# Loading W1 in three pieces, two scalings on ScalarE, logarithms recorded behind their sums, and matmuls of a group's halves ahead of its products

## The chip, the core and the metric

The kernel runs on one core of a Trainium2 chip. Its time is the device time of one execution in microseconds; lower is better. Before the change three runs gave 902.16, 903.32 and 903.46 us, median 903.32. The profile is of a fourth execution that took 901.05 us, of which the profiler's span covers 899.2 us.

## What is computed

`x` is 8 x 4224 tokens of 192 channels, `weight_gen` 8 x 4224 x 8 heads x 7 taps. W1 is 192 x 768 and W2 768 x 192, both in float64 words.

```python
w = exp(weight_gen - max(weight_gen, -1)); w = w / (sum(w, -1) + 1e-9)      # softmax over 7 taps
y[b, s, h] = sum_k w[b, s, h, k] * x_padded[b, s + k, h]                     # causal conv, 24 channels a head
xn = (y - mean(y)) / sqrt(var(y) + 1e-6) * g_ln                             # over 192 channels
out = y + maximum(xn @ w_ch1, 0) @ w_ch2
```

## The kernel before

**Tiling.** A partition holds 264 consecutive tokens of one sequence, so one token column is 128 tokens. Columns are worked off in parts of 4, 8 or 12 (six parts of 4 come first), each part in chunks of 4 or 6 columns for the convolution and in groups of 4 columns for the two matrix products: 66 groups.

**A chunk.** VectorE multiplies shifted `x` by the softmax weights, two taps at a time into `pr` (L423) or one into `y`. Two of the pairs are folded by accumulating DMAs that GpSimd issues (L429), and GpSimd adds the four remaining arrays into `y` (L426). ScalarE then sums and squares each column (L463, L468), takes the root by a logarithm and an exponential (L491 to L493), VectorE refines it (L496 to L502), ScalarE scales (`xh`, L514), rounds to float16 (L530), and GpSimd makes the low half (L532). Both halves of a group are `hl`; one DMA on the SP queue transposes them into `xT` (L536).

**A group on TensorE.** Three units of 16 + 4 matmuls of 256 columns (L546) give the hidden layer in a PSUM tile `ph` (there are two). A unit's 4 "narrow" matmuls stand in an instruction group of their own, shared by two units. ScalarE takes the positive part (`hh`, L576), VectorE the low half (`hlo`, L578), and TensorE multiplies by W2 in four output columns `o0` to `o3` of 18 matmuls each (L615 to L617). The outputs of a group stand between the units of the next group. VectorE adds them to `y` (L628), and a DMA writes the chunk.

**Softmax.** Its weights, sums (`sm`, written at L368) and some helper columns all lie in one PSUM tile, `wn`. ScalarE reads the sums for the logarithm (L372, "log" below) and turns it into a reciprocal (L373), VectorE refines that (L378, L379) and multiplies (L384). There are 23 softmax blocks.

**Weights.** W1's first 128 rows come by one DMA into `hh0`, its last 64 rows by another into `hh1` with a pattern of two column halves, 64 rows, 768 words (L660), W2 by a third into a `pr` buffer (L666). VectorE and ScalarE turn the words into float32 (L686 to L702); a matmul against ones gives the norm (L709), and from it come the scalings `gi` of W1 (L754) and `fs` of the output (L800). `gi` is needed for the float16 halves of W1 (L764, L767), which twelve small DMAs spread over partitions (L770).

**What sets the order.** Every operation is recorded with an engine, a cost, a due time (`WANT`) and its reads and writes. `Plan.order` places one after another, and the kernel's instructions are issued in the order of the starts it found, engine by engine in order. Waits between engines are derived from the order in which the instructions are issued; two instructions of different engines on one PSUM tile are kept apart even if both only read. DMAs of SP and ScalarE share eight semaphores in turn (DMAHW0 to DMAHW7); one waits until the transfer that used its semaphore before has landed.

Of the kernel before, what the change touches and what calls it, by code (L numbers as in the profile page):

```python
# [12 lines left out]
ALU = mybir.AluOpType  # L13
# [10 lines left out]
CHUNK = 6  # L24
RING = 36
HALF = 512
TINY = struct.unpack("<f", struct.pack("<I", (1023 - 126) << 20))[0]


# [35 lines left out]
class Plan:  # L65
# [42 lines left out]
    def order(self):  # L108
        tenant = {p: [None] * len(t) for p, t in self.pools.items()}
        free, cand, dma_free, out = {}, {}, {}, []  # L110

        last, clear = {"add": None, "turn": None}, {"add": 0.0, "turn": 0.0}
        for o in self.ops:
            o.left = len(o.deps)
            for d in o.deps:
                d.nxt.append(o)
            cand.setdefault(o.eng, [])
            free[o.eng] = 750.0
            if not o.left:
                cand[o.eng].append(o)  # L120

        def vacant(b):
            at = []
            for i, t in enumerate(tenant[b.pool]):
                if t is None:
                    at.append((0.0, i))
                elif all(x.end is not None for x in t.ops):
                    at.append((max(x.end for x in t.ops), i))
            return min(at) if at else None

        def earliest(o):
            t = max(free[o.eng], o.ready)
            if o.kind in clear:
                t = max(t, clear[o.kind])
            for b in o.bufs:
                if b.slot is None:
                    v = vacant(b) if b.ops[0] is o else None
                    if v is None:
                        return None
                    t = max(t, v[0])  # L140
            return t


        for o in reversed(self.ops):
            for d in o.deps:
                d.want = min(d.want, o.want)
        by_want, lead = sorted(self.ops, key=lambda o: o.want), 0
        while len(out) < len(self.ops):
            pick = None
            while by_want[lead].start is not None:  # L150
                lead += 1
            until, near = by_want[lead].want + WINDOW, by_want[lead].want + NEAR
            for e, c in cand.items():
                rows = [(t, o) for t, o in ((earliest(o), o) for o in c
                                          if o.want <= (near if o.kind == "load" else until))
                        if t is not None]
                if rows:
                    t0 = min(t for t, _ in rows) + AHEAD
                    row = min((r for r in rows if r[0] <= t0), key=lambda r: (r[1].want, r[1].rank))
                    if pick is None or row[0] < pick[0]:  # L160
                        pick = row
            assert pick is not None, "nothing can be placed"
            t, o = pick
            for b in o.bufs:
                if b.slot is None:
                    b.slot = vacant(b)[1]
                    tenant[b.pool][b.slot] = b
            o.start = t
            free[o.eng] = t + o.cost
            o.end = t + o.cost + o.lat  # L170
            if o.dma:

                begin = max(t + o.cost + self.DMA_START[o.kind if o.kind == "turn" else o.eng],
                            dma_free.get(o.eng, 0.0))
                dma_free[o.eng] = begin + o.dma * (1.0 if o.kind == "turn" else 1.2)
                o.end = dma_free[o.eng] + self.DMA_END
            if o.kind in clear:
                other = "turn" if o.kind == "add" else "add"
                o.behind, last[o.kind] = last[other], o
                clear[other] = max(clear[other], o.end)  # L180
            cand[o.eng].remove(o)
            for x in o.nxt:
                x.left -= 1
                x.ready = max(x.ready, o.end - (o.lat if x.eng == o.eng == "PE" else 0.0))
                if not x.left:
                    cand[x.eng].append(x)
            out.append(o)
        return sorted(out, key=lambda o: (o.start, o.rank))


@with_exitstack
def kernel(
# [66 lines left out]
    def a_ns(n, more=93):  # L259
        return n / 1.2 + more  # L260
# [28 lines left out]
        s0 += n  # L289
    parts, chunks, s0 = [], [], 0  # L290
    for n in PARTS:
        pa = dict(S=s0, n=n, chunks=[], xT={})
        o = 0
        while o < n:
            m = min(CHUNK, n - o) if n % CHUNK == 0 else min(4, n - o)
            so = max((q for q in softs if q["S"] <= s0 + o), key=lambda q: q["S"])
            assert s0 + o + m <= so["S"] + so["n"] and (s0 + o) // RING == (s0 + o + m - 1) // RING
            ch = dict(S=s0 + o, o=o, n=m, part=pa, so=s0 + o - so["S"])
            chunks.append(ch)
            pa["chunks"].append(ch)  # L300
            o += m
        parts.append(pa)
        s0 += n
# [40 lines left out]
    def softmax(pa):  # L344
# [9 lines left out]

        sm = WN[:, S0_ : S0_ + m]

        def step(eng, cost, name, fn, r, w):
            op(eng, cost, (name, S0), fn, r, w)

        step("V", v_ns(m * K), "max",  # L360
             lambda: V.tensor_reduce(out=at(mx)[:, :m], in_=a3(), axis=AX.X, op=ALU.max), [wb], [mx])
# [10 lines left out]
            A.activation(at(rr)[:, :m], sm, AF.Ln, bias=bias[:, 1:2])  # L372
            A.activation(at(rr)[:, :m], at(rr)[:, :m], AF.Exp, scale=-1.0)  # L373

        step("ACT", 2 * a_ns(m, 180), "rcp", ln, ["sm"], [rr])

        def newton():
            V.scalar_tensor_tensor(out=sm, in0=sm, scalar=1e-9, in1=at(rr)[:, :m], op0=ALU.add, op1=ALU.mult)  # L378
# [74 lines left out]
    def norm(pa):  # L453
# [52 lines left out]

        for g in range(0, n, NT):
            xh, hl, xT = Buf("xh"), Buf("hl"), Buf("xT")
            pa["xT"][g] = xT

            def scaled(j, g=g, xh=xh):
                for t in range(j, j + 2):
# [53 lines left out]
    def at_unit(unit):  # L566
        gp, u = unit
        return gp["s"] + u * NT / 3

    def evict(unit):  # L570
# [11 lines left out]
        if gp["prev"]:  # L582
            for t in ((0,), (1,), (2, 3))[u]:
                output(gp["prev"], t, gp["s"])

    def products(a, b):
        for gp, u in (a, b):
            gp["ph"][u] = Buf("ph")
        xs = [a[0]["xT"], b[0]["xT"]]
        pa_, pb_ = (gp["ph"][u] for gp, u in (a, b))  # L590
        op("PE", 1744, ("unit", at_unit(a)), lambda: wide_products(*a, True), [xs[0], *W1S], [pa_], lat=420.0)
        op("PE", 640, ("narrow", at_unit(b)), lambda: narrow_products(a, b), [*xs, *W1S], [pa_, pb_], lat=80.0)
        evict(a)
        op("PE", 1744, ("unit", at_unit(b)), lambda: wide_products(*b, False), [xs[1], *W1S], [pb_], lat=420.0)
        evict(b)
# [55 lines left out]
    def words(i, o, n):  # L651
        return at(raw[i]).bitcast(I32).rearrange("p a b d -> p (a b d)" if i == 2 else "p j q -> p (j q)")[:, o : o + n]

    def load_weights():

        def dma(eng, E, want, dst, src, n, w):
            op(eng, 450, ("w_" + want, 0), lambda: E.dma_start(dst(), src), w=[w], dma=dma_ns(n), kind="load")

        dma("SP", SY, "load", lambda: words(0, 0, 2 * F), w1b[0:P, :], 8 * F, raw[0])
        dma("SP", SY, "load", lambda: words(1, 0, F),  # L660
            bass.AP(tensor=w1b.tensor, offset=P * 2 * F, ap=[[F, 2], [2 * F, 64], [1, F]]), 4 * F, raw[1])
        dma("ACT", A, "load", lambda: W["g"][:, 0:1], gcol[0:P, :], 200, "g0")
        for h, rows in (("t", top), ("b", bot)):
            dma("ACT", A, "load", lambda rows=rows: W["g"][rows, 1:2], gcol[P:D, :], 100, "g1" + h)
        wv2 = w2b.rearrange("(j p) d -> p j d", p=P)
        dma("SP", SY, "load2", lambda: words(2, 0, 2 * NF * D).rearrange("p (j d) -> p j d", d=2 * D), wv2,  # L666
            8 * NF * D, raw[2])
# [60 lines left out]
    def weights():  # L728
# [9 lines left out]
            return at(b).bitcast(F32).rearrange("p j q -> p (j q)")[:, o : o + n]  # L738

        from_double("a", lambda: words(0, 0, 2 * F), lambda: f32(wa, F), F, s1[:, 0:1], [raw[0]], [wa])  # L740
        from_double("c", lambda: words(1, 0, F), lambda: f32(wc, F2), F2, s1[:, 1:2], [raw[1]], [wc])
        want = ("w_s1", 0)

        def gsum():
# [5 lines left out]

        op("V", 580, want, gsum, [(wa, "sq"), (wc, "sq"), "g0", "g1t", "g1b"], ["s1"])
        w_scale("s1", s1[:, 2:3], 128.0, r1, ["s1"], "r1")
        op("V", 130, want,
           lambda: V.tensor_scalar(out=gi, in0=g, scalar1=r1[:, 2:3], scalar2=None, op0=ALU.mult),  # L754
           ["r1"], ["gi"])


# [34 lines left out]
        for h in range(3):  # L792
# [3 lines left out]
        op("V", 70, want2, lambda: V.tensor_reduce(out=s2[:, 3:4], in_=s2[:, 0:3], axis=AX.X, op=ALU.add),  # L796
           [((w2r, h), "sq") for h in range(3)], ["s2"])
        w_scale("s2", s2[:, 3:4], 16384.0, r2, ["s2"], "r2")
        op("V", 130, want2,
           lambda: V.scalar_tensor_tensor(out=W["fs"], in0=r1[:, 1:2], scalar=1.0 / ALPHA, in1=r2[:, 1:2],  # L800
                                          op0=ALU.mult, op1=ALU.mult), ["r1", "r2"], ["fs"])
        w2f, w2g = (a.rearrange("p j d -> p (j d)") for a in (w2h, w2l))
        wv = [(w2r, h) for h in range(3)]
        op("ACT", a_ns(NF * D, 186), want2,
# [23 lines left out]
    prev, units = None, []  # L828
    for pa in parts:
        for g in range(0, pa["n"], NT):  # L830
            prev = dict(hh=Buf("hh"), hlo=Buf("hlo"), pa=pa, g=g, s=pa["S"] + g, xT=pa["xT"][g], ph={}, prev=prev)
            units += [(prev, u) for u in range(3)]
    for a, b in zip(units[::2], units[1::2]):
        products(a, b)
# [37 lines left out]
```

## Time and profile before

| | |
|---|---|
| runs | 902.16, 903.32, 903.46 us |
| profiled execution | 901.05 us, span 899.2 us |
| TensorE (PE) | 813.2 us busy, 90% |
| VectorE (DVE) | 781.7 us, 87% |
| GpSimd (POOL) | 694.4 us, 77% |
| ScalarE (ACT) | 675.7 us, 75% |
| granted TensorE clock, mean | 0.991 of full speed |

All five engines work most of the time, so the share of busy time says little by itself. What a place is worth is read from the stretch: before 53 us TensorE has nothing to multiply; after 82 us it hardly ever stands.

### The profile page before, as it was taken

To read this page: it belongs to the slowest core of one execution; us is meant where nothing else is said; L and a number is where in the kernel's file an instruction comes from. 1 tells how busy PE (TensorE), PEld (TensorE's weight loads), DVE (VectorE), ACT (ScalarE), POOL (GpSimd) and SP (SyncE) were. 2 spreads that over 40 slices of the span, in tenths; PEclk is the share of its full clock that TensorE was granted. 3 is DMA by queue.
4 is the path that set the end of the run, shared out by engine and by line. 5 is a ranking of instruction groups with operands and counts; after the bars stand their busy time and mean duration, and the time that the engine had idled before them with its cause. 6 is when DMAs were issued, how large, how long until landed. Compare 5 with 4: busy or idle time off the path is not lost.

```text
span 899.2 us, 21468 instructions
## 1 busy us (share of the span) xinstructions
PE 813.2 (90%) x8716; PEld 728.8 (81%) x8716; DVE 781.7 (87%) x833; ACT 675.7 (75%) x1773; POOL 694.4 (77%) x403
## 2 busy tenths in 40 slices
PE   0037979999999999989999999999999999999997
PEld 0025969889898888888899988898899898889987
DVE  5799989999999999889999998999999799785332
ACT  1579877888878787788878778788788778788321
POOL 4499989998998896886987979689698598886000
PEclk9997999999999999999999999999999999999999
DMA  8875778878786878777788688787877867654212
GB/s 212 211 166 126 173 160 180 195 163 189 164 195 111 203 147 193 184 158 166 164 187 185 139 182 175 169 197 158 170 167 148 170 134 162 153 111 98 63 53 54
DMA packets 138604, 142.42 MB, mean 158 GB/s; under 512 B 107657, under 2 KB 109449, under 8 KB 138505
## 3 DMA queue, kind: packets, MB, share of 16 engines
q1 hardware_dynamic: 123513, 89.14, 42.0%
q0 software_dynamic: 14688, 51.91, 29.6%
q8 instruction: 68, 1.11, 0.5%
q14 instruction: 31, 0.25, 0.1%
q10 hardware_dynamic: 304, 0.00, 0.0%
HBM read 36.43 MB, written 25.95 MB: 69 GB/s over the span
## 4 chain that ended last, share of the span: by engine, by line
PE 26%; DVE 12%; POOL 9%; ACT 8%; DMA 6%; issue 5%; SPq 0%; POOLq 0%; DVEq 0%
PE ph L546 13%; POOL y L426 7%; DVE pr L423 7%; PE po L615 5%; PE po L617 4%; PE po L616 4%; DMA xT<-hl 3%; DVE hlo L578 3%; ACT hh L576 3%; ACT junk L468 2%; DMA pr<-pr 2%; ACT junk L463 1%; DVE y L423 1%; POOL hl L532 1%; DVE y L628 1%
## 5 line engine op out<-in xcount | busy, mean ns | idle before, releaser
L426 POOL TENSOR_TENSOR y<-y,pr 128x1152 f32<-128x1152 f32 (+1 forms) x204 | 503.6, 2475 | 82.0 <-DVE pr L423 70.5
L616 PE MATMUL po<-c_w2l,hh 128*128 128x192 f16 x1584 | 389.7, 246 | 1.4 <-POOL c_w2l L808 1.4
L615 PE MATMUL po<-c_w2h,hh 128*128 128x192 f16 x1584 | 390.1, 246 | 0.0
L617 PE MATMUL po<-c_w2h,hlo 128*128 128x192 f16 x1584 | 389.7, 246 | 0.0
L546 PE MATMUL ph<-xT,c_w1h 128*128 128x256 f16 x2376 | 328.3, 275 | 34.2 <-DMA xT<-hl 18.8
L423 DVE TENSOR_TENSOR pr<-x,wn 128x2304 f32<-128x2304 f32 (+1 forms) x153 | 337.4, 2215 | 8.3 <-DMA x<-in_x_dram 3.3
L546 PEld LDWEIGHTS <-c_w1h 128*128 128x128 f16 x2376 | 226.4, 98 | 76.4 <-issue 43.2
L578 DVE SCALAR_TENSOR_TENSOR hlo<-ph,hh 128x1024 f16<-128x1024 f32 x198 | 239.3, 1217 | 49.9 <-ACT hh L576 48.7
L576 ACT ACTIVATE hh<-ph 128x1024 f16<-128x1024 f32 x198 | 199.6, 1008 | 68.8 <-PE ph L546 46.0
L546 PE MATMUL ph<-xT,c_w1l 128*128 128x256 f16 (+1 forms) x1584 | 211.0, 274 | 9.8 <-DMA xT<-hl 8.9
L615 PEld LDWEIGHTS <-hh 128*128 128x128 f16 x1584 | 155.0, 98 | 7.8 <-issue 6.1
L616 PEld LDWEIGHTS <-hh 128*128 128x128 f16 x1584 | 155.1, 98 | 1.6
L617 PEld LDWEIGHTS <-hlo 128*128 128x128 f16 x1584 | 155.0, 98 | 1.6 <-issue 1.6
L514 ACT ACTIVATE xh<-y,s 128x192 f32<-128x192 f32 x264 | 123.3, 536 | 31.9 <-DVE s L502 28.3
L546 PEld LDWEIGHTS <-c_w1l 128*128 128x128 f16 (+1 forms) x1584 | 108.5, 96 | 41.8 <-issue 26.2
L532 POOL TENSOR_TENSOR hl<-xh,hl 128x768 f16<-128x768 f32 x66 | 118.8, 1868 | 15.9 <-ACT hl L530 15.8
L463 ACT ACTIVATE junk<-y 128x192 f32<-128x192 f32 x264 | 95.1, 360 | 42.4 <-POOL y L426 36.8
L468 ACT ACTIVATE junk<-y,s 128x192 f32<-128x192 f32 x264 | 119.5, 453 | 7.1
L429 POOL DMA_DIRECT2D pr<-pr x102 | 96.2, 1003 | 34.5 <-DVE pr L423 20.9
L628 DVE SCALAR_TENSOR_TENSOR y<-po,c_fs,y 128x384 f32<-128x384 f32 x132 | 79.8, 608 | 28.2 <-PE po L617 28.1
L530 ACT ACTIVATE hl<-xh 128x768 f16<-128x768 f32 x66 | 55.1, 835 | 8.2 <-DMA xT<-hl 7.6
L423 DVE TENSOR_TENSOR y<-x,wn 128x1152 f32<-128x1152 f32 (+1 forms) x51 | 60.0, 1178 | 0.0
(64 smaller groups left out, 327.2 us busy)
## 6 DMA issues: line engine op xcount, KB each, us to landing
pr<-pr POOLq DMA_DIRECT2D x60, 576.0 KB, 7.6
x<-in_x_dram SPq DMA_DIRECT2D x30, 576.0 KB, 7.0
out_dram<-y SPq DMA_DIRECT2D x30, 576.0 KB, 4.8
pr<-pr POOLq DMA_DIRECT2D x42, 384.0 KB, 6.6
out_dram<-y SPq DMA_DIRECT2D x21, 384.0 KB, 4.3
x<-in_x_dram SPq DMA_DIRECT2D x20, 384.0 KB, 6.6
w<-in_weight_gen_dram SPq DMA_DIRECT2D x21, 336.0 KB, 4.3
pr<-in_moe_w_ch_dram SPq DMA_DIRECT2D x1, 1152.0 KB
```

The lines of the kernel that those rows point to most:

```text
L423: V.tensor_tensor(out=ov, in0=xv, in1=wv, op=ALU.mult)
L426: E.tensor_tensor(out=flat(0), in0=flat(0), in1=flat(k), op=ALU.add)
L463: A.activation(junk, at(y)[:, j, :], AF.Identity, scale=-1.0 / D, accum_out=at(s4)[:, 3, t : t + 1])
L468: A.activation(junk, at(y)[:, j, :], AF.Square, bias=at(s4)[:, 3, t : t + 1], accum_out=at(s4)[:, 0, t : t + 1])
L514: A.activation(at(xh)[:, t, :], at(y)[:, i, :], AF.Identity, bias=at(s4)[:, 3, g + t : g + t + 1], scale=at(s4)[:, 1, g + t : g + t + 1])
L532: lambda xh=xh, hl=hl: Q.tensor_tensor(out=halves(hl, True), in0=pairs(xh), in1=halves(hl, False), op=ALU.subtract),
L546: T_.matmul(at(gp["ph"][u])[:, r, v * 2 * P : (v + 1) * 2 * P], W[w][rows, wb, (2 * u + v) * P : (2 * u + v + 1) * P], xv[rows, r, xb, :, ...
L576: lambda: A.activation(at(hh)[:, us, :], at(ph), AF.Relu), [ph], [(hh, u)])
L578: lambda: V.scalar_tensor_tensor(out=at(hlo)[:, us, :], in0=at(ph), scalar=0.0, in1=at(hh)[:, us, :], op0=ALU.max, op1=ALU.subtract),
L615: T_.matmul(o, tok(hh, j), w2h[:, j, :], start=(j == 0), stop=False)
L616: T_.matmul(o, tok(hh, j), w2l[:, j, :], start=False, stop=False)
L617: T_.matmul(o, tok(hlo, j), w2h[:, j, :], start=False, stop=(j == NF - 1))
```

## The change

Six edits, in the order of the diff: (1) in the placed order, everything that neither the log needs nor its engine runs ahead of it is recorded behind the log instead of ahead of it (`hoist`); (2) logs are marked for that; (3) before the first unit of each of the first six groups TensorE multiplies the group's untransposed halves, 14 matmuls whose results are overwritten; (4) W1's last 64 rows come by two DMAs of 64 partitions; (5) `gi` moves from VectorE to ScalarE; (6) `fs` moves from VectorE to ScalarE, as two instructions.

```diff
+FILLED = 24
@@ Plan.order
-        return sorted(out, key=lambda o: (o.start, o.rank))
+        out.sort(key=lambda o: (o.start, o.rank))
+        return self.hoist(out)
+
+    @staticmethod
+    def hoist(out):
+        for o in [o for o in out if o.kind == "next"]:
+            j = out.index(o)
+            i = max(out.index(d) for d in o.deps) + 1
+            first, rest, tenants = [o], [], {(b.pool, b.slot) for b in o.bufs}
+            need, engines = set(o.deps), {o.eng}
+            for x in reversed(out[i:j]):
+                if x in need or x.eng in engines or x.dma or any((b.pool, b.slot) in tenants for b in x.bufs):
+                    first.append(x)
+                    need |= x.deps
+                    engines.add(x.eng)
+                    tenants |= {(b.pool, b.slot) for b in x.bufs}
+                else:
+                    rest.append(x)
+            out[i : j + 1] = first[::-1] + rest[::-1]
+        return out
@@ softmax
-        step("ACT", 2 * a_ns(m, 180), "rcp", ln, ["sm"], [rr])
+        step("ACT", 2 * a_ns(m, 180), "rcp", ln, ["sm"], [rr], kind="next")
@@ products
+    def fill(gp, u):
+        if gp["s"] >= FILLED:
+            return [], lambda: None
+
+        def mm():
+            h = at(gp["hl"]).rearrange("p t a d -> p (t a d)")
+            for i in range(14):
+                T_.matmul(at(gp["ph"][u])[:, i % 2, : 2 * P], h[:, :P], h[:, 2 * P : 4 * P], start=True, stop=True)
+
+        return [(gp["hl"], 0), (gp["hl"], 1)], mm
...
-        op("PE", 1744, ("unit", at_unit(a)), lambda: wide_products(*a, True), [xs[0], *W1S], [pa_], lat=420.0)
-        op("PE", 640, ("narrow", at_unit(b)), lambda: narrow_products(a, b), [*xs, *W1S], [pa_, pb_], lat=80.0)
+        (fa, mma), (fb, mmb) = (fill(*x) if x[1] == 0 else ([], lambda: None) for x in (a, b))
+        def wide():
+            mma()
+            wide_products(*a, True)
+        def narrow():
+            mmb()
+            narrow_products(a, b)
+        op("PE", 1744, ("unit", at_unit(a)), wide, [xs[0], *W1S, *fa], [pa_], lat=420.0)
+        op("PE", 640, ("narrow", at_unit(b)), narrow, [*xs, *W1S, *fb], [pa_, pb_], lat=80.0)
@@ load_weights
-        dma("SP", SY, "load", lambda: words(1, 0, F),
-            bass.AP(tensor=w1b.tensor, offset=P * 2 * F, ap=[[F, 2], [2 * F, 64], [1, F]]), 4 * F, raw[1])
+        for h, rows in enumerate((top, bot)):
+            dma("SP", SY, "load", lambda rows=rows: words(1, 0, F)[rows],
+                bass.AP(tensor=w1b.tensor, offset=P * 2 * F + h * F, ap=[[2 * F, 64], [1, F]]), 2 * F, (raw[1], h))
@@ weights
-        op("V", 130, want,
-           lambda: V.tensor_scalar(out=gi, in0=g, scalar1=r1[:, 2:3], scalar2=None, op0=ALU.mult),
+        op("ACT", 230, want, lambda: A.activation(gi, g, AF.Copy, scale=r1[:, 2:3]),
            ["r1"], ["gi"])
...
-        op("V", 130, want2,
-           lambda: V.scalar_tensor_tensor(out=W["fs"], in0=r1[:, 1:2], scalar=1.0 / ALPHA, in1=r2[:, 1:2],
-                                          op0=ALU.mult, op1=ALU.mult), ["r1", "r2"], ["fs"])
+        def final_scale():
+            A.activation(W["fs"], r1[:, 1:2], AF.Copy, scale=1.0 / ALPHA)
+            A.activation(W["fs"], W["fs"], AF.Copy, scale=r2[:, 1:2])
+
+        op("ACT", 440, want2, final_scale, ["r1", "r2"], ["fs"])
```

The due times are unchanged, but with other costs and one more operation the planner places many operations otherwise. The orders of all engines differ in small swaps up to about TensorE's instruction 6,228 of 17,428 (some 370 us into the run) and agree behind it.

On the SP queue at the start, before the change (`hh0` and `hh1` are the two parts of W1, `w` the softmax inputs, `pr2` is W2; the brackets name what is waited for):

```order
L657 DMA hh0_88<-in_moe_w_ch1_dram 128x1536
L657 DMA hh1_89<-in_moe_w_ch1_dram 128x1x768
L341 DMA w0_64<-in_weight_gen_dram 128x1x672 [waits DMAHW1_49,DMAHW0_49,Pool_49]
L335 DMA x_63<-in_x_dram 128x1x768 [waits DMAHW3_49]
L335 DMA x_63<-in_x_dram 128x1x768 [waits DMAHW4_49]
L335 DMA x_63<-in_x_dram 128x1x768 [waits DMAHW5_49]
L657 DMA pr2_78<-in_moe_w_ch2_dram 128x6x384 [waits DMAHW6_49]
```

And the same place of the changed program:

```order
L701 DMA hh0_88<-in_moe_w_ch1_dram 128x1536
L701 DMA hh1_89<-in_moe_w_ch1_dram 64x768
L701 DMA hh1_89<-in_moe_w_ch1_dram 64x768 [waits DMAHW1_49]
L362 DMA w0_64<-in_weight_gen_dram 128x1x672 [waits DMAHW3_49,DMAHW0_49,Pool_49]
L356 DMA x_63<-in_x_dram 128x1x768 [waits DMAHW4_49]
L356 DMA x_63<-in_x_dram 128x1x768 [waits DMAHW5_49]
L356 DMA x_63<-in_x_dram 128x1x768 [waits DMAHW6_49]
L701 DMA pr2_78<-in_moe_w_ch2_dram 128x6x384 [waits DMAHW7_49]
```

The second half of W1's last rows now stands ahead of `w0` and waits for the semaphore of the first load of `x`; each transfer behind it has moved on by one semaphore, so W2 waits no longer for `hh1` but for the first load of `g_ln`.

On VectorE around the third log (block `rr0`; `s40` is the first part's statistics, `y1` and `y2` are the second and third chunk), before:

```order
L423 TENSOR_TENSOR y1_68<-x_63,wn0_102 128x768
L754 TENSOR_SCALAR c_gi_115<-c_g_114,c_r1_118 128x2 [waits DVE_49]
L423 TENSOR_TENSOR pr3_79<-x_63,wn0_102 128x2x768 [waits Activation_49]
...
L502 TENSOR_TENSOR s40_98<-wn0_102,s40_98 128x4
L423 TENSOR_TENSOR pr1_77<-x_63,wn0_102 128x2x768 [waits DMASW1_49,Pool_49]
L423 TENSOR_TENSOR y2_69<-x_63,wn0_102 128x768
L378 SCALAR_TENSOR_TENSOR wn0_102<-wn0_102,rr0_94 128x96 [waits DVE_49]
```

And in the changed program:

```order
L444 TENSOR_TENSOR y1_68<-x_63,wn0_102 128x768
L444 TENSOR_TENSOR pr3_79<-x_63,wn0_102 128x2x768
...
L523 TENSOR_TENSOR s40_98<-wn0_102,s40_98 128x4
L444 TENSOR_TENSOR pr1_77<-x_63,wn0_102 128x2x768 [waits DMASW1_49,Activation_49,Pool_49]
L444 TENSOR_TENSOR y2_69<-x_63,wn0_102 128x768
L734 TENSOR_SCALAR po1_106<-pr2_78 128x384 [waits DMAHW7_49]
L399 SCALAR_TENSOR_TENSOR wn0_102<-wn0_102,rr0_94 128x96 [waits DVE_49,Activation_49]
```

The wait for ScalarE's log has moved from `pr3` to `pr1`; on ScalarE that log now stands behind the four `xh` of the first group, before it stood ahead of them.

On TensorE where the third group begins (`xT2` is its transposed input, `hl0` its halves), before:

```order
L616 MATMUL po1_106<-c_w2l_124,hh0_88 128x192
L617 LDWEIGHTS hlo0_90
L617 MATMUL po1_106<-c_w2h_123,hlo0_90 128x192
L546 LDWEIGHTS c_w1h_121
L546 MATMUL ph0_103<-xT2_87,c_w1h_121 128x256
```

And in the changed program, where the pair of instructions on `hl0` stands 14 times:

```order
L660 MATMUL po1_106<-c_w2l_124,hh0_88 128x192
L661 LDWEIGHTS hlo0_90
L661 MATMUL po1_106<-c_w2h_123,hlo0_90 128x192
L616 LDWEIGHTS hl0_83
L616 MATMUL ph0_103<-hl0_83 128x256
...
L567 LDWEIGHTS c_w1h_121
L567 MATMUL ph0_103<-xT2_87,c_w1h_121 128x256
```

The added matmuls are issued behind the previous group's output and ahead of the group's own products, whether the transposed input has arrived by then or not.

## Rows read from the trace of the kernel before

**Rows 1.** Windows by stage: us, busy (instructions) by engine, PEclk, DMA share, GB/s
```profile
53.02:81.57 28.55, 16.22 (x99) 11.00 (x99) 27.07 (x38) 25.77 (x77) 27.05 (x19) 0.76 0.75 162
81.57:126.60 45.03, 45.03 (x491) 40.64 (x490) 43.73 (x54) 35.71 (x98) 44.13 (x30) 1.00 0.69 152
126.60:133.60 7.00, 2.29 (x23) 1.72 (x22) 5.12 (x10) 5.90 (x17) 6.06 (x5) 1.00 0.78 190
133.60:182.00 48.40, 48.40 (x526) 43.75 (x526) 47.69 (x52) 37.97 (x106) 44.62 (x30) 1.00 0.88 186
182.00:300.00 118.00, 115.12 (x1247) 103.56 (x1245) 114.83 (x120) 101.40 (x270) 107.73 (x65) 1.00 0.77 169
300.00:370.00 70.00, 66.71 (x722) 59.87 (x720) 65.76 (x63) 55.75 (x148) 58.68 (x33) 1.00 0.76 162
450.00:800.00 350.00, 347.39 (x3759) 312.70 (x3757) 324.94 (x315) 283.16 (x744) 288.13 (x155) 1.00 0.76 163
```

**Rows 2.** Timeline 19 to 28 us: start, us, engine, line, operation [idle before, releaser]
```profile
26.75 0.40 SPq L657 DMA_DIRECT2D pr<-in_moe_w_ch_dram  x1
26.75 0.56 DVE L689 TENSOR_SCALAR ph<-hh 128x384 int32<-128x384 int32 x1 [7.12 <-DMA hh<-in_moe_w_ch_dram]
26.82 0.55 ACT L686 ACTIVATE pr<-hh 128x384 f32<-128x384 f32 x1 [9.02 <-DMA hh<-in_moe_w_ch_dram]
24.50 1.80 POOL L426 TENSOR_TENSOR y<-y,pr 128x768 f32<-128x768 f32 x1 [1.15 <-DMA pr<-pr]
```

**Rows 3.** Windows of 2 us in which W1's last rows arrive
```profile
20.00:22.00 2.00, 0.00 (x0) 0.00 (x0) 0.00 (x0) 0.00 (x0) 1.97 (x3) 1.00 0.97 249
24.00:26.00 2.00, 0.00 (x0) 0.00 (x0) 0.00 (x0) 0.00 (x0) 1.50 (x1) 1.00 0.13 52
```

**Rows 4.** DMA issues: operation, KB each, median us to landing; and the first loads' consumer
```profile
hh<-in_moe_w_ch_dram SPq DMA_DIRECT2D x1, 768.0 KB, 10.3
4.34 1.23 SPq L657 DMA_DIRECT2D hh<-in_moe_w_ch_dram  x2
9.95 3.42 DVE L423 TENSOR_TENSOR pr<-x,wn 128x1536 f32<-128x1536 f32 x2 [3.25 <-DMA x<-in_x_dram]
```

**Rows 5.** Timeline: ScalarE and VectorE from the first sums to the first group
```profile
31.38 0.35 ACT L463 ACTIVATE junk<-y 128x192 f32<-128x192 f32 x1
39.12 0.22 DVE L754 TENSOR_SCALAR c_gi<-c_g,c_r 128x2 f32<-128x2 f32 x1
39.24 0.34 ACT L372 ACTIVATE rr<-wn,bias 128x96 f32<-128x96 f32 x1 [1.50 <-DVE y L423]
39.61 1.75 DVE L423 TENSOR_TENSOR pr<-x,wn 128x1536 f32<-128x1536 f32 x1 [0.27 <-ACT rr L372]
43.13 1.85 ACT L514 ACTIVATE xh<-y,s 128x192 f32<-128x192 f32 x4
71.03 1.24 DVE L800 SCALAR_TENSOR_TENSOR c_fs<-c_r,c_r 128x1 f32<-128x1 f32 x1
128.28 1.75 DVE L423 TENSOR_TENSOR pr<-x,wn 128x1536 f32<-128x1536 f32 x1 [2.20 <-ACT rr L372]
```

**Rows 6.** Timeline of TensorE: starts of groups, and what it waited for
```profile
53.02 1.44 PE L546 MATMUL ph<-xT,c_w1h 128*128 128x256 f16 x6 [18.76 <-DMA xT<-hl]
70.01 0.61 PE L546 MATMUL ph<-xT,c_w1l 64*128 64x256 f16 x4 [6.03 <-DMA xT<-hl]
81.57 0.24 PE L616 MATMUL po<-c_w2l,hh 128*128 128x192 f16 x1 [1.38 <-POOL c_w2l L808]
83.61 0.83 PE L546 MATMUL ph<-xT,c_w1h 128*128 128x256 f16 x6
84.28 0.38 PE L546 MATMUL ph<-xT,c_w1l 128*128 128x256 f16 x2
128.17 0.39 PE L546 MATMUL ph<-xT,c_w1l 64*128 64x256 f16 x4 [1.56 <-DMA xT<-hl]
133.57 0.82 PE L546 MATMUL ph<-xT,c_w1h 128*128 128x256 f16 x6 [3.15 <-DVE hlo L578]
```

More of the change, by code (lines that the diff above doesn't have):

```diff
@@ L291 @@
     for n in PARTS:
-        pa = dict(S=s0, n=n, chunks=[], xT={})
+        pa = dict(S=s0, n=n, chunks=[], xT={}, hl={})
         o = 0
@@ L355, in softmax, with step @@
         sm = WN[:, S0_ : S0_ + m]
-        def step(eng, cost, name, fn, r, w):
-            op(eng, cost, (name, S0), fn, r, w)
+        def step(eng, cost, name, fn, r, w, **kw):
+            op(eng, cost, (name, S0), fn, r, w, **kw)
         step("V", v_ns(m * K), "max",
@@ L508, in norm @@
             xh, hl, xT = Buf("xh"), Buf("hl"), Buf("xT")
-            pa["xT"][g] = xT
+            pa["xT"][g], pa["hl"][g] = xT, hl
             def scaled(j, g=g, xh=xh):
@@ L740, in weights @@
         from_double("a", lambda: words(0, 0, 2 * F), lambda: f32(wa, F), F, s1[:, 0:1], [raw[0]], [wa])
-        from_double("c", lambda: words(1, 0, F), lambda: f32(wc, F2), F2, s1[:, 1:2], [raw[1]], [wc])
+        from_double("c", lambda: words(1, 0, F), lambda: f32(wc, F2), F2, s1[:, 1:2], [(raw[1], 0), (raw[1], 1)], [wc])
         want = ("w_s1", 0)
@@ L830 @@
         for g in range(0, pa["n"], NT):
-            prev = dict(hh=Buf("hh"), hlo=Buf("hlo"), pa=pa, g=g, s=pa["S"] + g, xT=pa["xT"][g], ph={}, prev=prev)
+            prev = dict(hh=Buf("hh"), hlo=Buf("hlo"), pa=pa, g=g, s=pa["S"] + g, xT=pa["xT"][g], hl=pa["hl"][g], ph={}, prev=prev)
             units += [(prev, u) for u in range(3)]
```

## The prediction

> **What bounds the kernel now.** I read the stages first, then what TensorE waits for, then the start. The stages [rows 1] show three regimes. From 53 to 82 us TensorE works 16.2 of 28.6 us, VectorE 27.1 and GpSimd 27.1: the first groups come as fast as these two make them. From 81.57 to 126.6 us TensorE works without a pause (45.03 of 45.03); it starts there when GpSimd has made W2's low half, 1.38 us late [rows 6]. From 126.6 to 133.6 us it stands 4.7 us: 1.56 us for the fifth group's transposed input, 3.15 us for a `ph` that VectorE empties late [rows 6]. Behind that it stands 0 us to 182, 2.9 us to 300, 3.3 us to 370 and 2.6 us from 450 to 800 [rows 1]. So the end is TensorE's start plus its work plus few pauses, and what the start gains or loses the end keeps, as long as the supply stays ahead.
>
> The start is a chain through W1. VectorE stands 7.12 us and ScalarE 9.02 us until W1's last rows land at 26.75 us [rows 2]. Meanwhile the DMA engines idle: at 20 to 22 us all are busy at 249 GB/s, at 24 to 26 us their share is 0.13 at 52 GB/s, which is 2 of 16 [rows 3]. The missing transfer runs on two engines, as its outermost dimension is 2.
>
> The page on DMA in the Trainium skill ("DMA: Bandwidth & Descriptors", section "Why a DMA increments its semaphore by 16 and not by 1") says that the number of engines is the largest divisor up to 16 of the slowest dimension; by that the old load has 2 engines and each new one, of 64 rows, 16. The share of 0.13 agrees for the old one; no row shows the new one.
>
> **The change part by part.** The sum is made against the profiled execution, 901.05 us; the median of the runs, 903.32, lies 2.27 above.
>
> *W1's last rows in two DMAs.* The 768 KB of W1's first rows land 10.3 us after 4.34, at 14.6 us [rows 4]. The first new half is queued right behind them. The second waits for the first load of `x`, which VectorE uses at 9.95 [rows 4], so it is issued where `w0` stood, and `w0` 0.6 us later, which no engine waits for before 24 us. Two halves of 196.6 kB at 249 GB/s [rows 3] take 1.6 us: landed at 16 to 17.5 us, and VectorE asks at 19.63 (26.75 less 7.12). The wait of 7.1 us goes; at worst, where two halves land no earlier than the whole, 0 goes. Next late is the first chunk: GpSimd finishes it at 26.3 us [rows 2], and ScalarE's sums, which begin at 31.38 [rows 5], can move by 5.1 us only. But ScalarE then catches up: before, its first W1 copy also waited for the log of 39.24 us behind 1.50 us of waiting [rows 5], and that log now comes later. W2, issued at 26.75 behind the old load [rows 2], goes out about 10 us earlier; nobody stood for it. I take **-7.1**, bounds 0 and -7.1.
>
> *gi and fs on ScalarE.* VectorE loses 0.22 and 1.24 us [rows 5] in the stage in which it works 27.1 of 28.6 us: **-1.5**. ScalarE gets three operations of some 0.2 us on a stretch where it works 25.8 of 28.6; `gi` replaces VectorE's on the path at the same price, `fs` is read first by an output. Bounds 0 and -1.5.
>
> *Logs recorded behind their sums.* No order of any engine changes by this, only who waits for whom. A log no longer waits for the convolution product that happened to be issued ahead of it (1.50 us at 39.24 us); the next product waits for the log instead. Before, VectorE paid 0.27 us at 39.61 and 2.20 us at 128.28 [rows 5]. In the new order `pr1` must wait for the third log, which stands on ScalarE behind four `xh` (1.85 us, [rows 5]) that themselves wait for VectorE's statistics just ahead of `pr1`. VectorE has nothing else there: it stands 1.85 + 0.34 = **+2.2**. At the fourth log ScalarE should arrive as VectorE finishes the sum: 0. Bounds: 0, if ScalarE is early, and 2.2 at each of the logs that changes (below).
>
> *Matmuls of the halves.* 84 matmuls. At full clock six start within 0.67 us (83.61 to 84.28, [rows 6]), 0.11 each, so a set of 14 costs 1.54 us where TensorE is late, and nothing where it waits. Groups one and two: TensorE waits 18.76 and 6.03 us for the transposition [rows 6]: free. Groups three to five: TensorE comes late, its work from 81.57 to 126.6 has no pause [rows 1]: 3 x 1.54 = 4.6. Group six 1.54 more. Against these 6.2 us stand the 1.56 and 3.15 us that TensorE now waits at 128 and 133 us [rows 6], which a later TensorE doesn't pay: **+1.5** net. Bounds 0 (all hidden) and +6.2 (the pauses come back, since VectorE and ScalarE get the hidden layer later).
>
> *The clock.* Granted are 0.76 of full speed from 53 to 82 us [rows 1], that is 1.2 GHz for parts of it and 2.4 for the rest; six matmuls take 1.44 us at 53.02 and 0.83 at 83.61 [rows 6], after TensorE had stood. The added matmuls give it work while it stood, but between their end and the products it stands again, since 14 at 1.2 GHz take some 3.4 us (1.44 / 6 each) and the transposition more. Of the two first groups only the second's first unit lies on the path to W2's low half (ScalarE evicts it ahead of that copy); 20 matmuls at half the time are 20 x 0.11 = 2.2 us at most. I take 0, bounds 0 and -2.2.
>
> *The new order.* TensorE's pauses between 182 and 370 us, 6.2 us, may vanish or double as operations swap; I take 0 and keep 6.2 both ways.
>
> **Sum:** -7.1 - 1.5 + 2.2 + 1.5 = -4.9. 901.05 - 4.9 = 896.15, and 2.27 to the median: **898.4 us**.
>
> **Rivals.** *The whole start arrives.* VectorE doesn't stand for the third log, the added matmuls hide in pauses and keep the clock up: -7.1 - 1.5 - 2.2 = -10.8, 892.5 us. For it: TensorE's two long waits in front of the first two groups [rows 6]. Against: 45 us without a pause right behind them.
>
> *The gain is given back.* The 6.2 us of added matmuls are paid in full, the pauses at 128 and 133 us come back beside them: -7.1 - 1.5 + 2.2 + 6.2 = -0.2, 903.1 us. For it: TensorE's 45.03 of 45.03 us. Against: those two pauses are waits for other engines, which a later TensorE shortens.
>
> *The load isn't quicker.* The same page, in "Rules for kernel authors", calls two transfers to disjoint partition halves useless, as they share the engines and run one after the other; one over 128 partitions is advised. The mechanism here would be that W1's last rows land at 26.7 us again: of the sum remain -1.5 + 2.2 + 1.5 = +2.2, 905.5 us. Against it the share of 0.13 [rows 3]: the old load has engines to gain.
>
> *VectorE stands for the logs* (the other side, slower). Every product on `wn` behind a hoisted log waits until ScalarE has come to that log; ScalarE is in order and has squares, evictions and scalings in front. Of the 23 logs 8 wait for a product in the old program and 2 in the new; at 6 logs the wait changes sides. The price is the 2.20 us at 128.28 [rows 5]. From the fourth such log on (4 x 2.2 = 8.8) it eats the 8.6 us that load and scalings bring; at all six it is 13.2 - 8.6 + 1.5 = +6.1, 909.4 us. For it: VectorE works 114.8 of 118 us from 182 to 300 [rows 1] and can't catch up. Against: in old steady state most products already stand so, and VectorE waited there only twice.
>
> The page "PSUM — Partial Sum Buffer", section "PSUM bank collisions raise a hardware error", demands such waits between two engines on one bank even for two reads; the 0.27 and 2.20 us agree, as product and log both only read `wn`.
>
> **How the numbers follow.** Forecast 0.50, the whole start 0.17, given back 0.12, load not quicker 0.05, logs 0.16. The likeliest case by itself reaches from 895 to 901.4. A measurement tells 0.2% (1.8 us) from no change. Faster (under 901.5): 0.49 of the forecast and 0.17 of the whole start, 0.66. Same: the gain given back 0.12, the rest of the forecast 0.01, of the load's case 0.02 and of the logs' case, where four or five are paid, 0.03: 0.18. Slower: 0.03 of the load's and 0.13 of the logs' case, 0.16. The range 892 to 905.5 takes in the first three cases and leaves out most of the logs' one.
>
> **What would show it.** Right: VectorE's wait at its L734 gone and the DMA share near 1 until W1 has landed by 18 us; VectorE standing about 2 us in front of `pr1` for L393; the first products near 46 us; TensorE's first output 4 to 6 us ahead of 81.57; the added matmuls of groups three to five without a wait behind them; the pauses at 128 and 133 us smaller. Wrong: W1's halves landing past 20 us, VectorE waiting for L393 in many places, or TensorE standing more than 12 us between 134 and 450 us.

## The result, and the profile after

The change makes the kernel slower: 905.48 us median of 16 runs (903.99 to 908.49) against 902.64 of the kernel before (900.82 to 904.14), ratio 1.0036 with a 95% interval of 1.0026 to 1.0046, some 3.3 us (the medians themselves lie 2.8 us apart). The forecast was 898.4 us. The profiled execution took 906.96 us, span 905.2, 5.9 us more than that of before; so the two profiles lie further apart than the runs do.

By stages, in the columns of [rows 1] (us, then busy time and instructions of PE, PEld, DVE, ACT, POOL, then clock, DMA share, GB/s); the last row has no counterpart there and stands below it for the kernel before:

```profile
53.02:81.57 28.55, 18.10 (x116) 13.19 (x116) 25.37 (x35) 22.70 (x62) 26.44 (x19) 0.76 0.58 115
81.57:126.60 45.03, 42.67 (x459) 38.80 (x456) 38.02 (x50) 33.12 (x93) 38.98 (x27) 1.00 0.71 148
126.60:133.60 7.00, 6.70 (x72) 5.78 (x71) 5.69 (x7) 3.95 (x13) 6.40 (x6) 1.00 0.68 156
133.60:182.00 48.40, 46.48 (x498) 41.21 (x498) 46.04 (x51) 37.96 (x104) 40.40 (x28) 1.00 0.75 163
182.00:300.00 118.00, 110.56 (x1163) 98.70 (x1161) 108.88 (x116) 92.18 (x243) 101.22 (x62) 0.97 0.75 162
300.00:370.00 70.00, 66.30 (x717) 59.60 (x715) 67.14 (x64) 60.60 (x162) 63.77 (x35) 1.00 0.80 177
450.00:800.00 350.00, 348.63 (x3780) 314.64 (x3778) 325.55 (x315) 284.20 (x752) 292.04 (x155) 1.00 0.75 165
370.00:450.00 80.00, 79.95 (x868) 72.13 (x866) 74.89 (x74) 64.76 (x171) 65.55 (x35) 1.00 0.82 174
```

```profile
370.00:450.00 80.00, 77.52 (x831) 69.22 (x831) 72.14 (x70) 64.75 (x170) 66.19 (x35) 1.00 0.80 179
```

TensorE is no longer busy all the time from 81.57 to 126.6 us, where VectorE works 38.02 us instead of 43.73, and from 182 to 300 us it stands 7.4 us instead of 2.9, at a granted clock of 0.97 instead of 1.00.

The start did what was forecast. Three windows of the columns above, the two halves of W1's last rows among the DMA issues (KB each, median us to landing), then the start on the timeline (start, us, engine, line, operation, in brackets idle time and what ended it):

```profile
14.00:16.00 2.00, 0.00 (x0) 0.00 (x0) 1.92 (x2) 0.93 (x2) 1.03 (x2) 1.00 1.04 218
16.00:18.00 2.00, 0.00 (x0) 0.00 (x0) 1.97 (x3) 1.15 (x4) 1.92 (x2) 1.00 1.09 251
24.00:26.00 2.00, 0.00 (x0) 0.00 (x0) 2.00 (x3) 0.17 (x1) 2.00 (x2) 1.00 1.07 386
```

```profile
hh<-in_moe_w_ch_dram SPq DMA_DIRECT2D x2, 192.0 KB, 8.4
```

```profile
4.33 5.49 SPq L701 DMA_DIRECT2D hh<-in_moe_w_ch_dram  x3
19.05 0.55 DVE L734 TENSOR_SCALAR ph<-hh 128x384 int32<-128x384 int32 x1
37.39 0.32 ACT L393 ACTIVATE rr<-wn,bias 128x96 f32<-128x96 f32 x1
37.80 1.75 DVE L444 TENSOR_TENSOR pr<-x,wn 128x1536 f32<-128x1536 f32 x1 [2.21 <-issue]
40.66 3.15 PE L616 MATMUL ph<-hl 128*128 128x256 f16 x14 [12.69 <-POOL hl L553]
45.72 1.44 PE L567 MATMUL ph<-xT,c_w1h 128*128 128x256 f16 x6 [1.92 <-DMA xT<-hl]
75.95 0.32 PE L660 MATMUL po<-c_w2l,hh 128*128 128x192 f16 x1 [0.81 <-POOL c_w2l L854]
82.94 1.69 PE L616 MATMUL ph<-hl 128*128 128x256 f16 x14
```

VectorE takes up W1's last rows at 19.05 without a wait, where it stood 7.12 us [rows 2]: the halves land 10.0 and 6.8 us behind their issues, the second at 16.1 us, where the whole landed at 26.75. The share of the DMA engines near 1 doesn't show this by itself, as it was 1.03 and 1.07 in the first two windows before; what is gone is the stretch at 0.13 behind them [rows 3], where now, from 24 to 26 us, the share is 1.07. The first products start at 45.72 instead of 53.02, the first output at 75.95 instead of 81.57 [rows 6]: 5.6 us ahead. VectorE stands 2.21 us for the third log, as forecast.

The lead is lost behind that. The fifth log and what it holds up:

```profile
91.78 1.03 ACT L597 ACTIVATE hh<-ph 128x1024 f16<-128x1024 f32 x1 [0.78 <-PE ph L567]
93.73 0.32 ACT L393 ACTIVATE rr<-wn,bias 128x96 f32<-128x96 f32 x1
94.14 1.75 DVE L444 TENSOR_TENSOR pr<-x,wn 128x1536 f32<-128x1536 f32 x1 [3.48 <-ACT rr L393]
97.08 0.81 PE L567 MATMUL ph<-xT,c_w1h 128*128 128x256 f16 x6 [2.36 <-DVE hlo L599]
100.88 1.02 ACT L597 ACTIVATE hh<-ph 128x1024 f16<-128x1024 f32 x1 [5.20 <-PE ph L567]
```

VectorE's next product waits for a log that stands on ScalarE behind an eviction (`hh`, ScalarE's reading of a `ph`), which itself waits for TensorE, and behind squares. VectorE's `hlo` comes late by that, TensorE waits 2.36 us for it, and ScalarE then 5.20 us for TensorE: a ring through three engines. The eighth log does it again, behind six scalings `xh` and two more, an eviction and two roundings:

```profile
210.74 2.73 ACT L535 ACTIVATE xh<-y,s 128x192 f32<-128x192 f32 x6
214.98 1.00 ACT L597 ACTIVATE hh<-ph 128x1024 f16<-128x1024 f32 x1
216.61 0.33 ACT L393 ACTIVATE rr<-wn,bias 128x96 f32<-128x96 f32 x1
217.03 3.42 DVE L444 TENSOR_TENSOR pr<-x,wn 128x1536 f32<-128x1536 f32 x2 [4.87 <-issue]
222.16 0.39 PE L567 MATMUL ph<-xT,c_w1l 64*128 64x256 f16 x4 [3.79 <-DVE hlo L599]
```

The profile names "issue" and not the log there, but the product starts 0.09 us after the log's end. VectorE's six waits for logs are 2.21, 0.56, 3.48, 0.47, 1.53 and 4.87, 13.1 us.

Between the two lies another pause of TensorE, of 3.65 us. It isn't the logs' work: with no log recorded behind its sum (a_no_hoist, below) a pause of 3.32 us stands in the same place. First the changed kernel, then a_no_hoist:

```profile
188.69 1.32 PE L567 MATMUL ph<-xT,c_w1h 128*128 128x256 f16 x6 [3.65 <-DVE hlo L599]
181.94 1.12 PE L567 MATMUL ph<-xT,c_w1h 128*128 128x256 f16 x6 [3.32 <-DVE hlo L599]
```

TensorE's account from its first output to 300 us: 5.6 ahead; four sets of added matmuls behind the second group, each 1.5 us (the third set, above, starts at 82.94 and the products behind it at 84.47) +6.1; pauses of 12.0 us against 7.6 in the kernel before +4.4; a clock 3% lower over 118 us +3.5: together +8.4. From 300 to 800 us it stands 5.1 instead of 8.4 us, -3.3. That accounts for 5.1 of the 5.9 us, but the account is rough, as it sets stretches of the clock against each other and not the same work: matched matmul by matmul, the added ones left out, TensorE is 10 to 12 us behind the kernel before at 300 us and 6.0 at the end. Why it makes up ground there was not tested.

### The profile page after: what moved, and what is told of

It is laid out like the page before. It is cut to its first block, busy times and chain, and to the rows that moved or that the text cites. A ratio compares the mean times of both kernels' runs of the same rounds, so it can differ in the third digit from the quotient of the medians.

```text
span 905.2 us, 21646 instructions
## 1 busy us (share of the span) xinstructions
PE 828.5 (92%) x8800; PEld 741.5 (82%) x8800; DVE 783.0 (87%) x831; ACT 676.9 (75%) x1776; POOL 694.6 (77%) x403
## 4 chain that ended last, share of the span: by engine, by line
PE 44%; DVE 8%; DMA 4%; ACT 2%; issue 2%; POOL 2%; SPq 0%; DVEq 0%; POOLq 0%
PE ph L567 22%; PE po L659 7%; PE po L661 7%; PE po L660 7%; DVE pr L444 4%; DMA pr<-pr 3%; DVE hlo L599 2%; POOL y L447 1%; DMA xT<-hl 1%; ACT hh L597 1%; DVE y L672 1%; DVE y L444 1%; ACT junk L489 1%; POOL pr L450 0%; ACT junk L484 0%
```

## The experiments

Three theories on where the lead goes: L, VectorE stands for the hoisted logs; M, TensorE pays for the added matmuls; O, the planner's other order. Every kernel was compared in 5 rounds with the kernel before on the same chip. "Changed" is the changed kernel, ratio 1.0036. Rows 1 to 4, 5 to 8, 9 to 11 and 12 to 14 of the table were each run on one occasion, on a chip of their own; across occasions the ratios are compared. The edits leave each engine's order as it is, but for what they add or take out.

| | edit | us | ratio | interval |
|---|---|---|---|---|
| a_no_hoist | changed, no log hoisted | 899.99 | 0.9980 | 0.9968 to 0.9992 |
| a_no_fill | changed, no added matmuls | 901.31 | 0.9998 | 0.9987 to 1.0009 |
| a_neither | both | 896.08 | 0.9942 | 0.9929 to 0.9955 |
| a_sums_sbuf | changed, sums in a tile of their own | 936.19 | 1.0387 | 1.0368 to 1.0406 |
| b_load | before, two DMAs for W1's last rows | 895.91 | 0.9918 | 0.9895 to 0.9940 |
| b_hoist | before, logs hoisted | 916.83 | 1.0159 | 1.0139 to 1.0179 |
| b_fill | before, added matmuls | 902.40 | 1.0003 | 0.9989 to 1.0018 |
| n_old_load | a_neither, W1's last rows in one DMA | 902.92 | 1.0000 | 0.9986 to 1.0014 |
| n_two_fills | a_neither, sets of groups one and two | 895.20 | 0.9910 | 0.9892 to 0.9928 |
| n_scalings_dve | a_neither, `gi` and `fs` on VectorE | 896.04 | 0.9920 | 0.9904 to 0.9936 |
| b_load_late | b_load, logs recorded late | 897.28 | 0.9942 | 0.9920 to 0.9966 |
| a_hoist_but_two | changed, fifth and eighth log not hoisted | 901.35 | 0.9986 | 0.9970 to 1.0001 |
| a_hoist_two | changed, only these two hoisted | 904.57 | 1.0017 | 1.0001 to 1.0034 |
| b_fill_28 | b_fill, 28 a set for groups three to six | 906.42 | 1.0048 | 1.0028 to 1.0069 |

**The logs, undone.**

```diff
-        step("ACT", 2 * a_ns(m, 180), "rcp", ln, ["sm"], [rr], kind="next")
+        step("ACT", 2 * a_ns(m, 180), "rcp", ln, ["sm"], [rr])
```

> The changed kernel, with the logs recorded again where the planner puts them; no engine's order differs. Theory L (VectorE stands for the logs): the six waits of VectorE in front of products (2.21, 0.56, 3.48, 0.47, 1.53 and 4.87 us, 13.1 together) mostly go, and of TensorE's pauses those of 2.36 us at 97 us and 3.79 us at 222 us; 905.5 falls by 5 to 10, to about 897. Theory M (the added matmuls: TensorE pays 1.54 us for each set from the third group on, and everything behind it comes later): within 2 us of 905.5. Theory O (the planner's other order up to 370 us): within 2 us of 905.5 too.

0.56% (5 us) come back. On VectorE the products at the same two places follow without a wait:

```profile
87.39 1.74 DVE L444 TENSOR_TENSOR pr<-x,wn 128x1536 f32<-128x1536 f32 x1
211.28 3.41 DVE L444 TENSOR_TENSOR pr<-x,wn 128x1536 f32<-128x1536 f32 x2
```

**The added matmuls, undone, and both.** `range(14)` becomes `range(0)`; then with the logs as above.

> The changed kernel without the 84 added matmuls; what else TensorE does, and all other engines, stands in the same order. Theory M: 4 sets of 1.54 us and the pauses behind them go, 905.5 falls by 6, to about 899. Theory L: TensorE comes earlier but waits for VectorE all the same: VectorE's wait of 3.48 us at 94 us shrinks by about 1.5 (the log stands behind evictions that wait for TensorE), that of 4.87 us at 217 us stays; 903 to 905. Theory O: 905.

> The changed kernel with the logs recorded where the planner puts them, and without the added matmuls. What is left is the load in two pieces, the scalings on ScalarE and the other order. L and M together: 905.5 - 8 - 6, about 892, near the 892.5 of the forecast's 'whole start'. L alone: 897; M alone: 899. Theory O: above 902.

The added matmuls cost 0.38%, 3.4 us, less than the 6.2 that theory M had; a_no_hoist against a_neither gives the same 0.38% with no log hoisted. The two costs add up: 0.56 + 0.38 = 0.94%, and with both undone the ratio falls by 0.94%. So L and M both hold, and O falls.

**Sums outside the PSUM tile.**

```diff
+    SM = cp.tile([P, MMAX], F32, name="sm")
...
-        sm = WN[:, S0_ : S0_ + m]
+        sm = SM[:, :m]
```

> The changed kernel with all its parts, but the softmax sums lie in a tile of their own outside the PSUM tile of the weights, so that a log waits for its sum alone and no product waits for a log. Theory L: VectorE's waits for logs are gone (under 0.5 us in front of any product), and the time is that of the run with the logs where the planner puts them or 1 to 3 us less, 894 to 897. Theory M and O: 903 to 906.

No product of VectorE waits for a log, and still the time is 34 us over that of before; all three theories missed it. The groups of VectorE's operations on the sums (shapes, count, busy us, mean ns, idle before them), here, and below in the changed kernel:

```profile
L400 DVE SCALAR_TENSOR_TENSOR sm<-sm,rr 128x96 f32<-128x96 f32 x21 | 43.7, 2083 | 0.0
L401 DVE SCALAR_TENSOR_TENSOR sm<-sm,rr 128x96 f32<-128x96 f32 x21 | 18.4, 874 | 0.7
L406 DVE TENSOR_TENSOR wn<-e,sm 128x672 f32<-128x672 f32 x21 | 24.9, 1188 | 0.0
```

```profile
L399 DVE SCALAR_TENSOR_TENSOR wn<-wn,rr 128x96 f32<-128x96 f32 x21 | 5.4, 256 | 0.1
L400 DVE SCALAR_TENSOR_TENSOR wn<-wn,rr 128x96 f32<-128x96 f32 x21 | 5.6, 266 | 0.7
L405 DVE TENSOR_TENSOR wn<-e,wn 128x672 f32<-128x672 f32 x21 | 17.9, 853 | 0.0
```

An operation of 256 ns takes 2083; the three together take 58 us more of VectorE. The experiment shows that the tile makes the waits, but its time says nothing on their price.

**Each part on the kernel before.** b_load issues two DMAs of 64 partitions where the single one stood; b_hoist has the changed kernel's `hoist`; b_fill the 14 matmuls ahead of each of the first six groups.

```diff
-        dma("SP", SY, "load", lambda: words(1, 0, F),
-            bass.AP(tensor=w1b.tensor, offset=P * 2 * F, ap=[[F, 2], [2 * F, 64], [1, F]]), 4 * F, raw[1])
+        def halves_of_w1():
+            for h, rows in enumerate((slice(0, 64), slice(64, P))):
+                SY.dma_start(words(1, 0, F)[rows],
+                             bass.AP(tensor=w1b.tensor, offset=P * 2 * F + h * F, ap=[[2 * F, 64], [1, F]]))
...
```

> The kernel before, with W1's last rows in two DMAs issued where the single one stood; nothing else differs in any order. Theory S (the faster load is what the changed kernel without logs and added matmuls has gained, 902.0 to 896.1): 896 to 898, VectorE's wait of 7.12 us gone, first products 5 to 7 us ahead of 53.02. Theory O (the gain of 5.9 lies in the planner's other order): 900 to 902.

> The changed kernel without hoisted logs and without added matmuls (896.1), but with W1's last rows in one DMA as before. Theory S: 901 to 903, VectorE waiting 6 to 7 us for W1 again. Theory O: 896 to 898.

S holds twice: by itself the load gives 0.82% (medians 902.83 and 895.91, 6.9 us), and a_neither loses 0.58% (5.2 us) without it; VectorE stands 6.92 us for W1 there again. What remains of the change, the two scalings and the planner's other order, is together worth nothing (n_old_load, 1.0000).

> The kernel before, with only the logs recorded behind their sums; no engine's order differs. Theory L (a log behind its sum makes the products wait, whatever the order): 902.0 + 4 to 6, 906 to 908, with VectorE waiting for logs in at least four places. Rival P (it hurts only where this program has TensorE early and VectorE short of time): within 2 of 902.

It costs 14 us, far more than L had, and P falls: the old program is hurt most. VectorE's waits for logs sum to 13.9 us there (2.53, 0.90, 0.75, 4.40 and 5.32), hardly more than the 13.1 of the changed kernel, where they cost 5; so their sum doesn't tell the price, and why it is so much higher here stays open. Its two longest waits, with the log ahead of the first and TensorE's pause behind the second:

```profile
214.36 0.32 ACT L392 ACTIVATE rr<-wn,bias 128x96 f32<-128x96 f32 x1
214.78 1.75 DVE L443 TENSOR_TENSOR pr<-x,wn 128x1536 f32<-128x1536 f32 x1 [4.40 <-ACT rr L392]
255.87 2.55 DVE L443 TENSOR_TENSOR pr<-x,wn 128x2304 f32<-128x2304 f32 x1 [5.32 <-ACT rr L392]
259.62 1.44 PE L566 MATMUL ph<-xT,c_w1h 128*128 128x256 f16 x6 [5.63 <-DVE hlo L598]
```

> The kernel before, with only the added matmuls. Theory M (sets three to six, 1.54 us each, are paid in part, 3.4 to 3.9 us as in the changed kernel): 905.4 to 905.9. Rival C (they keep the clock up in front of the first groups, which pays for them): 900 to 902, with the granted clock of 53 to 82 us above 0.76.

The added matmuls cost nothing there (0.03%, interval 0.15 either way), but not by C alone: in 81.57 to 126.6 us TensorE is as busy as before at a clock of 0.96, and its pauses of 1.56 and 3.15 us [rows 6] are gone:

```profile
53.02:81.57 28.55, 18.60 (x116) 12.57 (x115) 27.08 (x38) 24.89 (x73) 27.27 (x19) 0.82 0.80 162
81.57:126.60 45.03, 45.03 (x470) 40.21 (x468) 40.36 (x50) 35.10 (x95) 42.58 (x29) 0.96 0.66 148
126.60:133.60 7.00, 7.00 (x77) 6.47 (x77) 6.24 (x10) 4.03 (x17) 6.77 (x6) 1.00 0.66 170
```

**Which sets, which logs.** In n_two_fills the matmuls return where `gp["s"] >= 8`; in b_fill_28 groups three to six have 28; in the other two the hoist's list leaves out, or keeps only, the logs numbered 4 and 7 from 0.

> The changed kernel without hoisted logs (896.1 without any added matmul, 900.0 with all), with the added matmuls of the first two groups only. Theory M: these two sets lie in TensorE's waits of 18.42 and 8.30 us and cost nothing, 895.5 to 896.7, and the 3.9 us are those of groups three to six. Rival C (the clock stays up over the transposition): 893 to 895, with the first products of group one at 0.83 us for six instead of 1.44. Rival W (the halves come free later, so ScalarE's next halves wait): 897 to 899.

The first two sets cost nothing. Six first products took 0.81 us in that run and 1.44 in others with the same sets; whether the 0.9 us below a_neither are a gain stays open, since the two were timed on different occasions and their intervals lie side by side.

> The kernel before with the added matmuls, 28 instead of 14 in front of groups three to six: 56 more, 6.2 us by TensorE's clock. Theory P (the old program's pauses of 1.56 and 3.15 us and the 6.2 us behind them take the first 6.2 us, and what is more is paid): 907 to 909. Rival V (the old program is bound by VectorE there, so that TensorE has room for both): 902 to 904.

0.45% more (4 us) for 6.2 us of matmuls: P is nearer than V. Whether part of the second half is still hidden can't be told, as the two intervals leave the 4 us open by some 2 us either way.

> The changed kernel with all logs hoisted but the fifth and the eighth, those behind VectorE's waits of 3.48 us at 94 us and 4.87 us at 217 us; no engine's order differs. Theory L2 (these two carry the cost): 900 to 901.5, as without any hoist (900.0). Rival D (the cost is the sum of all six): 903 to 905.

> The changed kernel with the fifth and the eighth log hoisted alone. Theory L2: 904 to 905.5, as with all hoisted. Rival D: 901 to 902.5.

Two of 23 logs carry the loss: leaving them where they were gives back 0.50 of the 0.56%, hoisting them alone costs 0.37%. The rest, 0.06 to 0.19%, is for the other four waits, and these intervals don't tell it from nothing. The traces leave them a share at the start: TensorE's first output comes at 74.45 us with no log hoisted, at 74.92 with these two, at 75.63 with all but these two.

**The scalings, and logs recorded late.**

> The changed kernel without hoisted logs and added matmuls (896.1), with gi and fs written by VectorE again in the same places. The forecast's term: 1.5 us slower, 897.6. Rival (VectorE's 1.46 us there lie beside other waits): 895.5 to 896.7.

```diff
...
+            while not (out[k + 1].eng == o.eng or o in out[k + 1].deps
+                       or any((b.pool, b.slot) == (c.pool, c.slot) for b in out[k + 1].bufs for c in o.bufs)):
+                k += 1
+            out.insert(k, out.pop(j))
...
```

> The kernel before with W1's last rows in two DMAs (895.9), and each log recorded as late as ScalarE's order lets it, the reverse of the hoist; no engine's order differs. Theory L: VectorE's waits for logs (2.59 us at 122 us, 0.46 at 204) shrink, 893 to 895.5. Rival (ScalarE then waits for the product and evicts later, at the same price): 895.5 to 897.

Moving the scalings brings no gain that these runs show: the ratio is 0.9920 with them on VectorE and 0.9942 on ScalarE (a_neither), and the intervals overlap. On VectorE they took, in n_scalings_dve:

```profile
31.87 0.22 DVE L798 TENSOR_SCALAR c_gi<-c_g,c_r 128x2 f32<-128x2 f32 x1
64.52 0.15 DVE L844 SCALAR_TENSOR_TENSOR c_fs<-c_r,c_r 128x1 f32<-128x1 f32 x1
```

Recording logs late gives nothing either; its interval overlaps that of b_load.

The best versions, n_two_fills and b_load, are 0.8 to 0.9% faster than the kernel before. b_load is one edit.

## Why the prediction was wrong

The forecast was 4.9 us faster, and the kernel is some 3.3 us slower: the sign is wrong. Two of the signs of being wrong that the prediction named are there: VectorE waits for logs in six places, and TensorE stands 13.1 us between 134 and 450 us.

*W1's last rows, -7.1.* Right: -6.9 by itself, -5.2 beside the other parts. The Trainium skill's page "DMA: Bandwidth & Descriptors" calls two transfers to disjoint partition halves useless ("Rules for kernel authors"). Here they replace one that ran on two engines, and b_load shows the gain; the rule's comparison, with one transfer over 128 partitions, was not run.

*gi and fs, -1.5.* Wrong in size: no gain. The 0.22 us of `gi`, at 39.12 us, don't lie in the stage from 53 to 82 us to which the prediction counts them. The 1.24 us of `fs` [rows 5] were no work of VectorE's: the same operation took 0.15 above, and the last section shows what it stood beside.

*Logs behind their sums, +2.2.* This is the step that failed. The forecast found the one wait of 2.21 us exactly, and 0.56 at the fourth log where it had 0, but stopped there: it followed two logs and put all behind them at 0. The cost is 5 us, most of it from the fifth and the eighth log. It was the rival "VectorE stands for the logs", to which 0.16 were given, and its price was wrong too: 2.20 us a log, decided from the fourth on. In fact the waits run from 0.47 to 4.87 us, and two of them do most of it. A price read from one wait of the kernel before says nothing of a log that stands behind other work: what it costs is the work of ScalarE between the sum and the log, and an eviction there waits for TensorE, which waits for VectorE.

*Matmuls of the halves, +1.5.* Measured +3.4 to +3.9 in the changed kernel, 0 in the old one. The reasoning, 6.2 us less 4.7 of pauses, agrees with the old program (b_fill) within its interval. In the changed one TensorE starts 5.6 us earlier, and the pauses that were to shrink (1.56 and 3.15 us) are others (2.36, 3.65, 3.79 us). The term was netted against pauses of a program that no longer existed. The hoisted logs aren't the reason, as the matmuls cost the same 0.38% without them; whether it is the earlier start or the planner's order stays open, since the matmuls were not run on b_load.

*The clock, 0.* Right for the start, where it was counted: 0.76 from 53 to 82 us as before, six first products at 1.44 us. The 0.97 from 182 to 300 us, some 3.5 us in the account above, had no term.

*The new order, 0.* Right in sum, as n_old_load is at 1.0000, though single pauses moved, as that of 3.65 us shows.

With the measured sizes the sum is -5.2 + 5.0 + 3.4 = +3.2 us, which is what the change costs. The first figure is a_neither against n_old_load, so the sum rests on the two costs adding up, as they did above.

## What to carry to other kernels

A wait between two engines that only read the same tile can be turned round by the order of recording, but it doesn't go away while both use the tile: follow the instruction that now has to be reached, and add up what its engine does before it, above all work that waits for a third engine. Work out every place at which the wait turns, not the first two. Time each part of a bundle by itself; here one edit held all of the gain, and two took more than it back.

## What the runs showed of the hardware

*Where an operand lies sets its cost beside GpSimd.* With the sums in SBUF, VectorE's operation on two SBUF inputs took 2083 ns instead of 256. The page "SBUF — State Buffer" of the Trainium skill, section "Who interferes with whom", says that a VectorE instruction with two SBUF inputs contends with a GpSimd instruction that reads SBUF; the trace agrees. GpSimd works 75% of the time in that run. The operation took 0.25 us where GpSimd stood until 236.01, and 2.38 us where it began 0.36 us into an addition of GpSimd's, and there it ended 0.1 us behind that addition:

```profile
234.56 0.25 DVE L400 SCALAR_TENSOR_TENSOR sm<-sm,rr 128x96 f32<-128x96 f32 x1
236.01 2.29 POOL L448 TENSOR_TENSOR y<-y,pr 128x768 f32<-128x768 f32 x1 [4.99 <-DMA pr<-pr]
383.24 2.63 POOL L448 TENSOR_TENSOR y<-y,pr 128x1152 f32<-128x1152 f32 x1
383.60 2.38 DVE L400 SCALAR_TENSOR_TENSOR sm<-sm,rr 128x96 f32<-128x96 f32 x1
```

The operations that grew are those whose two inputs now both lie in SBUF; the sum itself, with one input, took 844 ns, and 858 in the changed kernel. The `fs` of the kernel before is the same case. It ran from 71.03 to 72.27 us [rows 5], beside an addition that ended at 72.26:

```profile
70.45 1.81 POOL L426 TENSOR_TENSOR y<-y,pr 128x768 f32<-128x768 f32 x1
```

*The clock behind a pause.* In the changed kernel, in windows of 2 us behind the pauses of 3.65 and 3.79 us:

```profile
188.00:190.00 2.00, 1.31 (x7) 0.95 (x7) 2.00 (x4) 1.42 (x5) 2.00 (x2) 0.71 0.11 20
190.00:192.00 2.00, 2.00 (x12) 1.44 (x10) 2.00 (x3) 1.76 (x7) 2.00 (x2) 0.50 0.00 0
224.00:226.00 2.00, 2.00 (x12) 1.54 (x11) 2.00 (x2) 0.31 (x1) 1.29 (x1) 0.50 1.01 259
```

TensorE runs at 1.2 GHz there, 12 matmuls in 2 us where it does 21.8 at 2.4 GHz (491 in 45.03 us [rows 1]), so these pauses of 3.7 us cost more than themselves. The length of a pause alone doesn't tell: behind that of 3.15 us in the kernel before [rows 6] the clock was 1.00, and behind one of 2.63 us in a_neither, at 123.9 us, six first products took 1.44 us, at 0.50 granted from 124 to 126 us:

```profile
123.90 1.44 PE L567 MATMUL ph<-xT,c_w1h 128*128 128x256 f16 x6 [2.63 <-DVE hlo L599]
```
